# Attention and MLP decode on one core: the last 64 rows of w2 move from a load beside wq into the K/V stream, as eight strided loads, and the last w1 block streams 4 columns instead of 64

## The chip, the cores and the metric

One core of a Trainium2 chip. The metric is the device time of one execution in microseconds (us). The profile's *span* runs from the first to the last recorded instruction and is 1.3 to 1.5 us shorter than the time in most runs; I call the difference, time less span, the **outside time**.

## The reference

```python
# x: 4 x 1 x 640; k_cache, v_cache: 4 x 32 x 4096 x 128 (bf16); wq 640 x 4096; wo 4096 x 640
# w1 640 x 1728; w2 1728 x 640
def _A_ref(x, k_cache, v_cache, wq, wo):          # cached attention, one query row a batch
    q = (x @ wq).reshape(B, Sq, H, Dh) ...
    scores = jnp.einsum("bhqd,bhkd->bhqk", q, k_cache) * (Dh ** -0.5)
    o = jnp.einsum("bhqk,bhkd->bhqd", softmax(scores), v_cache)
    return o ... @ wo
def _B_ref(x, w1, b1, w2):                        # mish MLP
    h = x @ w1 + b1
    return (h * jnp.tanh(softplus(h))) @ w2
h = x + _A_ref(layernorm(x), k_cache, v_cache, wq, wo)
out = h + _B_ref(layernorm(h), w1, b1, w2)
```

Nearly all of the bytes are K and V: 32 tiles of 8 MB out of 283 MB. F = 1728 is 13 blocks of 128 rows and a rest of 64; this rest (FT = 64 rows of w2, 80 KB) is what the change moves.

## The kernel before

`sp`, `ac`, `pe` and `dv` below are the programs of SyncE, ScalarE, TensorE (PE) and VectorE. `load(p, dst, src, key, sem)` starts a DMA on engine `p`; `need(key)` waits for it. Three 8 MB buffers (slots A, B, C) take the K and V tiles in turn, all from SP's queue.

```python
def first_loads():
    load(sp, slot["C"][:, 0 : DC * H * Dh], A_wq..., "wq", "WQ")      # 5.2 MB
    load(ac, x_bf[:, :], x_rows[:, :], "x", "X")
    load(ac, w2_tail[0:FT, :], B_w2[FM * P : F, :], "w2t", "WT")      # 64 rows x 1280 bytes
    k_load(0)
    k_load(1)

def sync_prog():
    for hg in range(NHG):
        i = hg * N
        ...                                                           # cut
        sp.need(("PV", i - 1) if hg else "b1p")                       # b1p: b1 transposed by PE
        v_load(i)
        sp.need(("F", i, NS - 1))
        k_load(i + 2)
        ...                                                           # cut: the other tiles, then wo, w1, w2
```

The end of PE's program: w1 in three column blocks (2, 2 and 1 of the five 128-row chunks of D), then the part of w2 that needs only the residual, then the w2 products. WD = 16 makes PE write each result 16 times (64 columns for 4 rows of data); only one copy is read. The extra columns keep PE busy: the last block's 14 products take 1.08 us with 64 columns at clock 0.5.

```python
    for c0, c1 in zip(W1S, W1S[1:]):                                  # (0,2) (2,4) (4,5)
        ...                                                           # cut: b1 before the last block
        pe.need(("w1", c0))
        for j in [FM] + list(range(FM)):
            for c in range(c0, c1):
                ...                                                   # cut: w is the 128 x 128 piece of w1
                mm(h1_w[0 : (P if j < FM else FT), j, :, :], w,
                   cen[:, c, :].unsqueeze(1).to_broadcast([P, WD, N]), False, done, ...)
    pe.need("h_lo", "h_hi")
    ...                                                               # cut: 40 small products, the residual
    pe.need("act")
    pe.need("w2t")
    w2_mm(FM)                                                         # the 64-row rest
    for j0, j1 in zip(W2S, W2S[1:]):                                  # blocks 0-3, 4-7, 8-11, 12
        pe.need(("w2", j0))
        for j in range(j0, j1):
            w2_mm(j)
```

The softmax here doesn't subtract the row's maximum and nothing guards it: scores larger than these inputs give would overflow.

Of the kernel before, what the change touches and what calls it, by code (L numbers as in the profile page):

```python
# [78 lines left out]
def kernel(  # L79
# [15 lines left out]
    N, _, D = A_x.shape  # L95
    _, H, Sk, Dh = A_k_cache.shape
    F = B_w1.shape[1]
    P = 128
    DC = D // P
# [8 lines left out]
    FM = F // P  # L108
    FT = F - FM * P
# [22 lines left out]
    def sb(name, shape, dt, region=at, top=SLOT0):  # L132
        size = 4 if dt == FP32 else 2
        for d in shape[1:]:
            size *= d
        size = -(-size // 32) * 32
        t = nc.alloc_sbuf_tensor_at(name, shape, dt, offset=region[0]).ap()
        region[0] += size
        assert region[0] <= top, (name, region[0])
        return t  # L140
# [29 lines left out]
    w2_tail = sb("w2_tail", (P, D), BF16)  # L170
# [32 lines left out]
    cen = sb("cen", (P, DC, N), BF16, tail, topA)  # L203
# [24 lines left out]
    WD = 16  # L228
# [9 lines left out]
    h1_w = red[:, 2:4, :].rearrange("p k (j w n) -> p (k j) w n", w=WD, n=N)  # L238
# [13 lines left out]
    sp = Prog(nc.sync, book)  # L252
    po = Prog(nc.gpsimd, book)
    ac = Prog(nc.scalar, book)
    dv = Prog(nc.vector, book)
    pe = Prog(nc.tensor, book, take=["DVP", "DVA", "ACP", "VA", "VC", "V2"] + WSEM + ["B0", "B1"])

    def tiles(src, i):
        hg, b = divmod(i, N)
        return src[b, hg * G : (hg + 1) * G].rearrange("h (q r) d -> (h q) (r d)", q=PG)  # L260

    def load(p, dst, src, key, sem):
        p.do(lambda: p.eng.dma_start(out=dst, in_=src), key, sem, 16)  # L263
# [22 lines left out]
    def k_load(i):  # L286
        c = KS[i % N]
        load(sp, slot[c][:, :], tiles(A_k_cache, i), ("K", i), "K" + c)

    def v_load(i):  # L290
        c = VS[i % N]
        src = tiles(A_v_cache, i)
        n = SLOT // 2 if i == NT - 1 else SLOT
        load(sp, slot[c][:, 0:n], src[:, 0:n], ("V", i), "V" + c)
        if n < SLOT:
            load(sp, slot[c][:, n:SLOT], src[:, n:SLOT], ("V2", i), "V2")
        elif i % N == N - 1:
            sp.signal(("V2", i), "V2", 16)

    def first_loads():  # L300
        load(
            sp, slot["C"][:, 0 : DC * H * Dh], A_wq.rearrange("(p c) n -> p (c n)", c=DC), "wq", "WQ"
        )
        load(ac, x_bf[:, :], x_rows[:, :], "x", "X")
        load(ac, w2_tail[0:FT, :], B_w2[FM * P : F, :], "w2t", "WT")
        k_load(0)
        k_load(1)

# [3 lines that stand above are left out]
            if hg:  # L312
                sp.need(("PV", i - 2))
                k_load(i)
                sp.need(("F", i - 1, NS - 1))
                k_load(i + 1)
            sp.need(("PV", i - 1) if hg else "b1p")
            v_load(i)
            sp.need(("F", i, NS - 1))
            k_load(i + 2)  # L320
            sp.need(("PV", i))
            v_load(i + 1)
            sp.need(("F", i + 1, NS - 1))
            k_load(i + 3)
            sp.need(("F", i + 2, NS - 1))
            v_load(i + 2)
            sp.need(("PV", i + 1))
            v_load(i + 3)
        sp.need(("F", NT - 1, NS - 1))
        for n, (q, j0, j1) in enumerate(WOS):  # L330
            load(
                sp, wo_sb[:, q, j0:j1, :],
                A_wo[q * QN : (q + 1) * QN, :].rearrange("(p j) n -> p j n", j=G)[:, j0:j1, :],
                ("wo", q, j0), f"W{n}",
            )
        w1_v = B_w1.rearrange("(p c) n -> p c n", c=DC)
        for k, (c0, c1) in enumerate(zip(W1S, W1S[1:])):
            load(sp, w1_sb[:, c0:c1, :], w1_v[:, c0:c1, :], ("w1", c0), f"W{len(WOS) + k}")
        sp.need(("PV", NT - 2))
        for k, (j0, j1) in enumerate(zip(W2S, W2S[1:])):  # L340
            load(
                sp, w2_sb[:, j0:j1, :],
                B_w2[j0 * P : j1 * P, :].rearrange("(p j) n -> p j n", j=j1 - j0), ("w2", j0),
                f"W{len(WOS) + len(W1S) - 1 + k}",
            )
        store(sp, 0)
        leave(sp, 0)
# [378 lines left out]
    def mm(out_, lhsT, rhs, start, stop, mark=None, skip=True):  # L726
        pe.do(
            lambda: nc.tensor.matmul(  # L728
                out_, lhsT=lhsT, rhs=rhs, start=start, stop=stop, skip_group_check=skip
            ),  # L730
            mark, "PE",
        )
# [100 lines left out]
    def l_mm(hg):  # L833
        pe.need(("rsm", hg))
        mm(l_ps, rsm[:, :, :].rearrange("p b g -> p (b g)"), ones[:, :], True, True, ("L", hg))
# [34 lines left out]
    def pe_tail():  # L870
        def wo_mm(k):
            pe.need(("a", k))
            for j in range(G):
                if (k, j) in [w[:2] for w in WOS]:
                    pe.need(("wo", k, j))
                for c in range(DC):
                    w = wo_sb[:, k, j, :].rearrange("p (m c) -> p c m", c=DC)[:, c, :]
                    done = k == NHG - 1 and j == G - 1 and c == DC - 1
                    mm(
                        y_w[:, c, :, :], w, a_t[:, k, j, :].unsqueeze(1).to_broadcast([P, WD, N]),  # L880
                        False, done, "y" if done else None,
                    )

        hg = NHG - 1
        pe.freeze()
        wo_mm(0)
        o_mm(NT - 1)
        l_mm(hg)
        wo_mm(1)
        a_mm(hg)  # L890
        pe.need("zeros", ("e", NT - 1, NS - 1))
        for k in (2, 3):
            mm(red[:, k, :], ident[:, :], zeros[:, 0:1].to_broadcast([P, 512]), True, False)
        mm(y2_ps, ident[:, :], zeros[:, 0:OC], True, False)
        wo_mm(2)
        wo_mm(3)
        pe.need("ysum")
        mm(m_ps, ones_d[:, :], ysum[:, :], True, True, "mean")
        pe.need("sq")
        mm(sq_ps, ones_d[:, :], sq[:, :, :].rearrange("p c n -> p (c n)"), True, True, "sqm")  # L900
        pe.need("cen")
        for c0, c1 in zip(W1S, W1S[1:]):
            if c1 == DC:
                pe.need("b1_lo")
                for part in (b1_hi, b1_lo):
                    for j0, j1 in ((0, FC // 2 + 1), (FC // 2 + 1, FC)):
                        mm(h1_ps[:, j0:j1, :], ident[:, :], part[:, j0:j1, :], False, False)
# [3 lines that stand above are left out]
                    if j < FB * FI:  # L911
                        k, i = divmod(j, FI)
                        w = w1_sb[:, c, k * FI * P : (k + 1) * FI * P]
                        w = w.rearrange("p (f i) -> p i f", i=FI)[:, i, :]
                    else:
                        w = w1_sb[:, c, j * P : min((j + 1) * P, F)]
                    done = c == DC - 1 and j == FM - 1
                    mm(
                        h1_w[0 : (P if j < FM else FT), j, :, :], w,
                        cen[:, c, :].unsqueeze(1).to_broadcast([P, WD, N]), False, done,  # L920
                        "h1_ps" if done else None,
                    )
        pe.need("h_lo", "h_hi")
        for part in (h_hi, h_lo):
            for k in range(CG):
                for c in range(DC):
                    mm(
                        y2_ps[k * QD : k * QD + N, :].rearrange("b (m c) -> b c m", c=DC)[:, c, :],
                        part[:, c, :], ident[:, k * QD : (k + 1) * QD], False, False,
                    )  # L930
        pe.need("act")

        def w2_mm(j):
            rows = P if j < FM else FT
            for k in range(CG):
                cs = slice(k * OC, (k + 1) * OC)
                done = j == FM - 1 and k == CG - 1
                mm(
                    y2_ps[k * QD : k * QD + N, :], act[0:rows, j, :],
                    w2_sb[:, j, cs] if j < FM else w2_tail[0:FT, cs], False, j == FM - 1,  # L940
                    "y2" if done else None,
                )

        pe.need("w2t")
        w2_mm(FM)
        for j0, j1 in zip(W2S, W2S[1:]):
            pe.need(("w2", j0))
            for j in range(j0, j1):
                w2_mm(j)
# [77 lines left out]
```

## Time and profile before

The first three runs gave a median of 661.48 us (661.27 to 661.50).

The page of the kernel before: its span, the granted TensorE clock (PEclk, tenths of full speed), the DMA rows over 40 equal slices, the queues (packets, MB, share; q1 is SP's, q10 is ACT's) and the chain of waits that ended last.

```profile
span 659.9 us, 4968 instructions
...
PEclk9768787979759697958767888788875879796968
DMA  9999999999999999999999999999999999999997
GB/s 387 445 445 441 434 406 437 442 441 434 430 417 445 437 437 433 437 417 445 433 441 433 437 417 445 433 437 438 433 421 445 429 437 441 433 421 445 415 416 324
...
q1 hardware_dynamic: 6784, 283.27, 99.4%
...
q10 hardware_dynamic: 112, 0.09, 0.0%
...
DMA 3%; SPq 2%; PE 1%; issue 0%; DVE 0%
DMA slotA<-in_B_w_dram 3%; SPq L263 2%; PE pv L728 1%; PE red L738 0%; PE red L728 0%; DVE o_bf L724 0%
```

The DMA row is full in 39 of 40 slices and the stream moves 429 to 430 GB/s; 27.1 GB/s for each of 16 DMA engines. The chain is the end of that stream. So the time is the stream, plus a start, plus a tail. Two loads, from the view of DMA issues (KB each, us from issue to landing):

```profile
slotC<-in_A_wq_dram SPq DMA_DIRECT2D x1, 5120.0 KB, 16.0
...
w_tail<-in_B_w_dram ACTq DMA_DIRECT2D x1, 80.0 KB, 13.3
```

The tail, from the timeline (start us, busy us, engine, line, operation, tile, shape, count, and in brackets the idle time before it and what ended it):

```profile
651.32 1.64 PE L728 MATMUL red<-cen,slotB 128*64 128x64 bf16 x28 [0.78 <-DMA slotB<-in_B_w_dram]
...
652.99 1.08 PE L728 MATMUL red<-cen,slotB 128*64 128x64 bf16 x14
...
655.65 0.22 DVE L717 SCALAR_TENSOR_TENSOR act<-tb,hm 128x56 bf16<-128x56 f32 x1
...
655.92 0.24 PE L728 MATMUL red<-w_tail,act 64*4 64x160 bf16 x4 [1.09 <-DVE act L717]
...
656.09 0.72 PE L728 MATMUL red<-slotA,act 128*4 128x160 bf16 x32
...
657.02 0.65 PE L728 MATMUL red<-slotA,act 128*4 128x160 bf16 x20 [0.21 <-DMA slotA<-in_B_w_dram]
...
657.73 0.32 DVE L724 CAST o_bf<-red 128x160 bf16<-128x160 f32 x1 [1.86 <-PE red L728]
```

`cen` products are w1's, `act` is the activation, `slotA,act` products are w2's, `o_bf` is the output copy. PE runs 32 w2 products, then waits for the last w2 loads. The chain says so too:

```profile
639.18 17.80 DMA slotA<-in_B_w_dram
...
657.02 0.68 PE red L728 x20
```

And the granted clock over the tail, from the view by windows (length, then busy time and count by engine, PEclk, DMA share, GB/s):

```profile
core 0: us, PE busy (x) PEld busy (x) DVE busy (x) ACT busy (x) POOL busy (x), PEclk, DMA share, GB/s
651.40:654.10 2.70, 2.70 (x54) 2.47 (x58) 0.00 (x0) 0.00 (x0) 0.00 (x0) 0.56 1.02 420
654.10:655.90 1.80, 0.73 (x40) 0.54 (x38) 1.54 (x6) 0.25 (x1) 0.00 (x0) 0.71 0.93 374
655.90:658.10 2.20, 1.54 (x56) 0.93 (x56) 0.32 (x1) 0.00 (x0) 0.00 (x0) 1.00 0.19 73
```

PEclk is 0.56 during the last w1 blocks and 1.00 during the w2 products.

Below I also use the trace's packet records, which no printed view lists one by one. Sorted by end, the 64 KB packets of K and V fall into groups of 16, one packet for each DMA engine, so the lag of every engine at every step can be read, although the engines carry no names. In this stream a group follows the last after 2.415 us, within 0.01 us, except where an instruction fetch or a small load falls between: whatever an engine loses, it keeps to the end. The last w2 load therefore lands when the *slowest* engine has its share: first landing 655.70 us, last 657.39 us.

### The profile page before, as it was taken

The numbers are of one execution on the slowest core, as the hardware profiler recorded it, in microseconds if no ns is written. First come the engines' busy times: TensorE is split into PE (matmuls) and PEld (weight loads), VectorE is DVE, ScalarE is ACT, GpSimd is POOL, SyncE is SP. The second block draws the span as 40 slices with busy tenths as digits, with TensorE's granted clock in tenths as the row PEclk, the third lists the DMA queues.
The fourth block names the chain that finished last, engine by engine and source line by source line (L and its number), as shares of the span: only waits on it lengthen the run. The fifth ranks groups of instructions, "written<-read, shape, count | busy, mean of one in ns | idle before, by whom it ended". The sixth has DMA issues, their size and how long they took to land. (4 is left out here: it accounts for less than half of the span.)

```text
span 659.9 us, 4968 instructions
## 1 busy us (share of the span) xinstructions
PE 382.4 (58%) x2630; PEld 68.6 (10%) x1672; DVE 407.7 (62%) x257; ACT 40.7 (6%) x157; POOL 1.7 (0%) x12
## 2 busy tenths in 40 slices
PE   0356758556317595738417485848434757675766
PEld 0100000101101010101100010010110001010145
DVE  1077988495049778757208798849306798857702
ACT  0200000000000000000000000000000000000011
POOL 0000000000000000000000000000000000000000
PEclk9768787979759697958767888788875879796968
DMA  9999999999999999999999999999999999999997
GB/s 387 445 445 441 434 406 437 442 441 434 430 417 445 437 437 433 437 417 445 433 441 433 437 417 445 433 437 438 433 421 445 429 437 441 433 421 445 415 416 324
DMA packets 6905, 283.48 MB, mean 430 GB/s; under 512 B 809, under 2 KB 1136, under 8 KB 2160
## 3 DMA queue, kind: packets, MB, share of 16 engines
q1 hardware_dynamic: 6784, 283.27, 99.4%
q8 instruction: 6, 0.10, 0.1%
q10 hardware_dynamic: 112, 0.09, 0.0%
q14 instruction: 3, 0.02, 0.0%
HBM read 283.35 MB, written 0.01 MB: 429 GB/s over the span
## 5 line engine op out<-in xcount | busy, mean ns | idle before, releaser
L527 DVE TENSOR_TENSOR slotA<-slotA,q_bc 128x8192 bf16<-128x8192 bf16 x32 | 140.6, 4415 | 92.2 <-DMA slotA<-in_A_k_cache_dram 92.2
L527 DVE TENSOR_TENSOR slotB<-slotB,q_bc 128x8192 bf16<-128x8192 bf16 x32 | 140.7, 4416 | 16.2 <-DMA slotB<-in_A_k_cache_dram 16.2
L538 DVE TENSOR_REDUCE s_f<-red 128x64 f32<-128x1024 f32 x64 | 78.0, 1219 | 96.4 <-PE red L738 96.3
L738 PE MATMUL red<-slotA,ident 128*128 128x512 bf16 x480 | 137.3, 450 | 0.0
L738 PE MATMUL red<-slotB,ident 128*128 128x512 bf16 x480 | 124.5, 418 | 0.0
L728 PE MATMUL red<-slotA,ident 128*128 128x512 bf16 x32 | 14.5, 452 | 128.5 <-PEq L49 128.5
L728 PE MATMUL pv<-slotC,e 128*32 128x512 bf16 x768 | 51.9, 430 | 39.6 <-PEq L49 36.6
L728 PE MATMUL red<-slotB,ident 128*128 128x512 bf16 x32 | 14.0, 437 | 86.9 <-PEq L49 86.9
L404 ACT ACTIVATE ex<-s_f 128x64 bf16<-128x64 f32 x64 | 16.4, 256 | 511.4 <-DVE s_f L538 511.4
L552 DVE TENSOR_TENSOR e<-ex,hmask 128x512 bf16<-128x512 bf16 x64 | 39.8, 683 | 0.0
L728 PEld LDWEIGHTS pv<-slotC,e 128*32 128x32 bf16 x768 | 22.3, 107 | 97.7 <-issue 83.6
L728 PEld LDWEIGHTS red<-slotA,ident 128*128 128x128 bf16 x32 | 3.2, 99 | 197.2 <-issue 197.1
L728 PEld LDWEIGHTS red<-slotB,ident 128*128 128x128 bf16 x32 | 3.1, 98 | 169.0 <-issue 169.0
L728 PEld LDWEIGHTS o_ps<-pv_sb,selo 128*32 128x32 f32 x136 | 13.5, 109 | 63.6 <-issue 63.5
L728 PE MATMUL o_ps<-pv_sb,selo 128*32 128x128 f32 x136 | 18.0, 276 | 0.0
L728 PE MATMUL pv<-slotA,e 128*32 128x512 bf16 x256 | 14.5, 379 | 0.9 <-PEq L49 0.9
L414 ACT COPY pv_sb<-pv 128x512 f32<-128x512 f32 x16 | 9.4, 585 | 70.6 <-PE pv L728 70.6
L404 ACT ACTIVATION_READ_ACCUMULATOR ex<-s_f 128x1 f32 x64 | 11.9, 186 | 0.0
L577 DVE RECIPROCAL rl<-misc 32x1 f32<-32x1 f32 x4 | 0.6, 151 | 14.4 <-PE misc L728 14.4
L728 PEld LDWEIGHTS pv<-slotA,e 128*32 128x32 bf16 x256 | 7.1, 97 | 22.2 <-issue 16.6
L517 DVE CAST b1T<-pv 128x13 bf16<-128x13 f32 x1 | 0.2, 174 | 13.1 <-PE pv L728 13.1
L728 PE MATMUL red<-slotC,lnT 128*32 128x512 bf16 x40 | 4.4, 620 | 6.0 <-PEq L49 6.0
(105 smaller groups left out, 70.3 us busy)
## 6 DMA issues: line engine op xcount, KB each, us to landing
slotC<-in_A_v_cache_dram SPq DMA_DIRECT2D x2, 4096.0 KB, 40.5
slotC<-in_A_wq_dram SPq DMA_DIRECT2D x1, 5120.0 KB, 16.0
slotB<-in_A_wo_dram SPq DMA_DIRECT2D x3, 1280.0 KB, 17.7
slotA<-in_B_w_dram SPq DMA_DIRECT2D x3, 640.0 KB, 18.9
slotB<-in_B_w_dram SPq DMA_DIRECT2D x2, 864.0 KB, 24.4
slotB<-in_A_wo_dram SPq DMA_DIRECT2D x1, 640.0 KB, 21.4
slotB<-in_A_wo_dram SPq DMA_DIRECT2D x1, 480.0 KB, 22.1
slotB<-in_B_w_dram SPq DMA_DIRECT2D x1, 432.0 KB, 22.8
```

The costliest lines, as they stand in the source:

```text
L404: lambda: a.activation(out=ex[:, sl], in_=s_f[:, sl], func=ACT.Exp, scale=SCALE, accum_out=rs[:, b, s : s + 1],),
L414: lambda: a.copy(out=pv_sb[:, :, :].rearrange("p r d -> p (r d)"), in_=pv[:, :]),
L517: dv.do(lambda: v.tensor_copy(out=b1T[:, 0:FM], in_=b1_ps[:, 0:FM]), "b1m", DV)
L527: lambda: v.tensor_tensor(out=t, in0=t, in1=q_bc[:, hg, b, :].unsqueeze(1).to_broadcast([P, RS, Dh]), op=ALU.mult,),
L538: lambda: v.tensor_reduce(out=s_f[:, s * RS : (s + 1) * RS], in_=red[:, k : k + 2, :].rearrange("p k (r c) -> p (k r) c", c=CW), axis=AX.X ...
L552: lambda: v.tensor_tensor(out=e[:, sl, :], in0=ex[:, sl].unsqueeze(2).to_broadcast([P, RS, G]), in1=hmask[:, :].unsqueeze(1).to_broadcast( ...
L577: dv.do(lambda: v.reciprocal(out=rl[:, :], in_=l_ps), ("rl", hg), DV)
L728: lambda: nc.tensor.matmul(out_, lhsT=lhsT, rhs=rhs, start=start, stop=stop, skip_group_check=skip),
L738: return t.add_instruction(mybir.InstMatmult(name=nc.get_next_instruction_name(), engine=mybir.EngineType.PE, ins=[t.lower_ap(rhs), t.lowe ...
```

## The change

Intent: take the 80 KB away from the start, where they compete with wq, and load them later in the stream, in eight loads of eight rows, each at every fourth partition. And shorten PE's last w1 block, so that a shorter DMA stream isn't followed by PE work.

```diff
@@ first_loads
-        load(ac, w2_tail[0:FT, :], B_w2[FM * P : F, :], "w2t", "WT")
@@ sync_prog, after v_load(i)
+            if hg == 0:
+                for k in range(FT // 8):
+                    r = slice(k // 4 * 32 + k % 4, k // 4 * 32 + 32, 4)
+                    load(sp, w2_tail[r, :], B_w2[FM * P : F, :][r, :], ("w2t", k), "WT")
@@ last w1 block
+                    wd = WD if c1 < DC else 1
                     mm(
-                        h1_w[0 : (P if j < FM else FT), j, :, :], w,
-                        cen[:, c, :].unsqueeze(1).to_broadcast([P, WD, N]), False, done,
+                        h1_w[0 : (P if j < FM else FT), j, 0:wd, :], w,
+                        cen[:, c, :].unsqueeze(1).to_broadcast([P, wd, N]), False, done,
@@ before the w2 products
-        pe.need("w2t")
+        pe.need(("w2t", FT // 8 - 1))
```

## The prediction

> **What bounds the kernel.** The page shows 283.48 MB at 430 GB/s, the DMA row at 9 tenths in 39 of 40 slices; PE is busy 58%, DVE 62%. The trace's packet records, followed one by one, are sharper: from 1.2 to 657 us no DMA engine is without work, and every 64 KB packet of the K and V stream takes 2.418 us (27.1 GB/s an engine). So the span is start-up, the bytes of the *slowest* of 16 engines, and what follows the last landing. The chain of waits agrees: it ends in the w2 loads, then w2 products (0.68 us), output copy (0.32 us) and store. The engines are out of step: the last w2 load lands on its first engine 1.69 us before its last. Small loads of x and b1 leave three engines up to 1.2 us late, and each instruction fetch (8 or 16 KB, at 80, 97, 118, 147, 157, 176, 457 us) sets one engine back by about 0.6 to 1.5 us.
>
> **What changes.**
> 1. w2's last 80 KB leave the start. There every engine carried four 1280-byte packets, each 52 to 66 ns between two wq packets, plus a completion: about 0.25 us. All 16 engines should start the K stream that much earlier.
> 2. The same bytes come back behind V tile 0. [...] this trace can't name engines, but the four-row x load has four data landings. Those engines get eight packets and eight completions, estimated from the packets above at 0.42 to 0.5 us; the rest none. Net: engines 0 to 7 about +0.2 us, 8 to 15 about -0.25 us.
> 3. Eight more issues cost SP about 8 x 0.43 us near 23 us, where it next waits until about 60 us: free.
> 4. The 14 products of the last w1 block take 1.08 us at half clock with 64 columns; with 4 I estimate 0.5 us. But PE already waits for the last two w2 landings (idle 0.21 and 0.17 us before them), so this is off the path, or insurance should the DMA end earlier.
>
> **On the path.** Only the slowest engine counts. The four latest lie within 0.25 us. If all are among 8 to 15, the end moves by -0.25 us; if one is among 0 to 7, by 0 to +0.25 us. The trace does not say which; I take it as even. Fewer columns could also lower the granted clock for the w2 products (a few tenths of a us).
>
> **Prediction:** 661.35 us, eight times in ten within 660.8 to 661.9. Faster by over 2%: 1%; within 2%: 98%; slower: 1%.
>
> **What would show it.** wq lands about 0.2 us earlier; eight 10 KB loads on SP follow V tile 0; K landings shift by -0.2 us before them, half the engines by +0.2 afterwards; the last w1 products take about 0.5 us; PE idle before the last w2 landings grows to 0.5 us or more; the chain still ends in w2 loads.
>
> **What would make it wrong.** wq packets slow from 1.514 to 1.645 us at about 8 to 11.5 us on all engines at once; if w2's load causes this, another 0.3 us is won. Small packets that stall a 64 KB neighbour would cost more. Fetches that fall on other engines would move the maximum by up to 0.5 us.

"Those engines" and "engines 0 to 7" are the eight that I took to carry the eight loads, "8 to 15" the rest; the trace numbers none. The sum came to 0.13 us under the 661.48 us of before, which is even odds of -0.25 us and of about 0.

## The result

In the first comparison the changed kernel took 661.83 us (median of 6, 661.55 to 663.01), the kernel before 661.49 us (6 runs): ratio 1.0008, interval 0.9996 to 1.0021. A ratio here is the mean time of one kernel's fast runs over that of the other's of the same rounds, so not quite the ratio of the medians. Three repeats gave 1.0009, 1.0010 and 1.0004. Each interval holds 1; the four together say "slower by a few tenths of a us", against the 0.13 us faster that I forecast.

The page after:

```profile
span 660.2 us, 4975 instructions
...
PEclk9768787968659796868767887788876879797967
...
q1 hardware_dynamic: 6912, 283.35, 99.3%
...
q10 hardware_dynamic: 32, 0.01, 0.0%
...
DMA 4%; PE 2%; SPq 0%; DVE 0%; issue 0%; ACT 0%
DMA slotB<-in_B_w_dram 4%; PE red L731 1%; PE pv L731 1%; PE red L741 0%; SPq L263 0%; DVE tb L717 0%; DVE o_bf L727 0%; ACT ta L441 0%; DVE tb L706 0%; DVE h L694 0%; DVE act L720 0%; DVE tb L714 0%
```

The DMA issues after:

```profile
slotC<-in_A_wq_dram SPq DMA_DIRECT2D x1, 5120.0 KB, 15.5
...
w_tail<-in_B_w_dram SPq DMA_DIRECT2D x8, 10.0 KB
```

The first step of the forecast is there: wq lands 0.5 us sooner after its issue (15.5 for 16.0 us), and the eight 10 KB loads are on SP. The tail, from the timeline:

```profile
651.46 1.82 PE L731 MATMUL red<-cen,slotB 128*64 128x64 bf16 x28 [0.80 <-DMA slotB<-in_B_w_dram]
...
653.32 0.73 PE L731 MATMUL red<-cen,slotB 128*64 128x4 bf16 x14
...
655.63 0.22 DVE L720 SCALAR_TENSOR_TENSOR act<-tb,hm 128x56 bf16<-128x56 f32 x1
...
655.90 0.30 PE L731 MATMUL red<-w_tail,act 64*4 64x160 bf16 x4 [1.09 <-DVE act L720]
...
656.13 1.90 PE L731 MATMUL red<-slotA,act 128*4 128x160 bf16 x52
658.09 0.33 DVE L727 CAST o_bf<-red 128x160 bf16<-128x160 f32 x1 [2.24 <-PE red L731]
```

The chain:

```profile
626.18 25.24 DMA slotB<-in_B_w_dram
...
651.46 2.60 PE red L731 x46
...
655.90 2.16 PE red L731 x55
```

And the clock over the tail:

```profile
core 0: us, PE busy (x) PEld busy (x) DVE busy (x) ACT busy (x) POOL busy (x), PEclk, DMA share, GB/s
651.40:654.10 2.70, 2.64 (x55) 2.51 (x59) 0.01 (x1) 0.00 (x0) 0.00 (x0) 0.52 1.02 422
654.10:655.90 1.80, 0.71 (x40) 0.52 (x36) 1.52 (x6) 0.25 (x1) 0.00 (x0) 0.50 0.84 336
655.90:658.10 2.20, 2.14 (x56) 1.51 (x56) 0.01 (x1) 0.00 (x0) 0.00 (x0) 0.50 0.16 61
```

Three things are new. The last w1 block is shorter, 0.73 for 1.08 us, and yet the activation comes at the same time (655.63 and 655.65 us), because the second block started later and ran slower. The clock is then 0.50 where it was 1.00, and the 52 w2 products run for 1.90 us without waiting for the last loads: PE, not the stream, now ends the kernel, and the output copy starts at 658.09 instead of 657.73 us. And the chain, which was the w2 load followed by PE, is now the second w1 load followed by PE, ScalarE and VectorE. The last w2 landing itself moved by only 0.14 us, to 657.53 us.

That looks like a complete story, 0.36 us of it. It isn't: it is one profile of each kernel, and the repeats below show that the *spans* of the two kernels do not differ on average.

### The profile page after: what moved, and what is told of

It is laid out like the page before. It is cut to its first block, busy times and chain, and to the rows that moved or that the text cites. A ratio compares the mean times of both kernels' runs of the same rounds, so it can differ in the third digit from the quotient of the medians.

```text
span 660.2 us, 4975 instructions
## 1 busy us (share of the span) xinstructions
PE 388.8 (59%) x2630; PEld 69.5 (11%) x1672; DVE 407.8 (62%) x257; ACT 40.7 (6%) x157; POOL 1.7 (0%) x12
## 5 line engine op out<-in xcount | busy, mean ns | idle before, releaser
L741 PE MATMUL red<-slotA,ident 128*128 128x512 bf16 x480 | 140.4, 458 | 0.0
L741 PE MATMUL red<-slotB,ident 128*128 128x512 bf16 x480 | 126.1, 422 | 0.0
L731 PE MATMUL red<-slotA,ident 128*128 128x512 bf16 x32 | 14.3, 448 | 127.4 <-PEq L49 127.4
L731 PE MATMUL red<-slotB,ident 128*128 128x512 bf16 x32 | 14.1, 440 | 85.3 <-PEq L49 85.3
## 6 DMA issues: line engine op xcount, KB each, us to landing
slotC<-in_A_wq_dram SPq DMA_DIRECT2D x1, 5120.0 KB, 15.5
```

The source lines that it names most:

```text
L731: lambda: nc.tensor.matmul(out_, lhsT=lhsT, rhs=rhs, start=start, stop=stop, skip_group_check=skip),
L741: return t.add_instruction(mybir.InstMatmult(name=nc.get_next_instruction_name(), engine=mybir.EngineType.PE, ins=[t.lower_ap(rhs), t.lowe ...
```

## The experiments

All runs in one table. "Ratio" is to the kernel before in the same call. "Long" counts the runs with an outside time (time less span, 1.3 to 1.5 us in most runs) above 1.7 us. For the kernel before I pool 46 runs: mean time 661.77 us, mean span 660.26 us (659.7 to 661.0), 4 of 46 long; a 47th, of 822.84 us, was slow and is left out, and so are the six runs of the first comparison, for which no spans are on record. Spans are recorded to 0.1 us, so runs close to 1.7 us can fall on either side of that line.

| run | what | median us | ratio | spans us | long |
|---|---|---|---|---|---|
| after | the change | 661.83 | 1.0008 | 660.1 to 660.4 | 4 of 6 |
| r1 | the same | 662.51 | 1.0009 | 660.1 to 660.2 | 5 of 6 |
| r3 | the same | 661.93 | 1.0010 | 660.2 to 660.5 | 3 of 5 |
| r6 | the same | 661.68 | 1.0004 | 660.1 to 660.4 | 1 of 5 |
| e1 | stream, wide block | 661.62 | 1.0000 | 659.9 to 660.7 | 0 of 5 |
| r4 | the same | 661.94 | 1.0004 | 660.0 to 660.8 | 0 of 5 |
| e2 | narrow block only | 661.56 | 0.9998 | 660.1 to 660.3 | 0 of 5 |
| r5 | the same | 661.45 | 1.0001 | 659.9 to 660.5 | 0 of 5 |
| e3 | stream, one load | 661.60 | 0.9997 | 659.8 to 660.2 | 1 of 5 |
| e6 | stream, four loads | 661.32 | 0.9995 | 659.7 to 660.6 | 0 of 6 |
| e4 | rest not loaded | 661.35 | 0.9996 | 659.4 to 660.1 | 1 of 5 |
| e5 | start, eight loads | 666.22 | 1.0066 | 663.8 to 665.2 | 2 of 6 |
| e7 | start, before x | 661.78 | 1.0001 | 659.9 to 660.7 | 1 of 6 |
| f1 | changed, 24 spare products | 661.75 | 1.0003 | 660.2 to 660.4 | 0 of 5 |
| f3 | changed, 4 spare products | 661.72 | 0.9999 | 660.1 to 660.4 | 0 of 5 |
| f2 | before, 20 products fewer | 661.64 | 0.9999 | 659.8 to 660.5 | 0 of 5 |
| g1 | four loads, wide, 14 spare wide products | 661.15 | 0.9991 | 659.7 to 659.9 | 0 of 5 |
| g2 | the same | 661.13 | 0.9989 | 659.6 to 660.1 | 0 of 5 |
| g3 | before, 14 spare wide products | 661.33 | 0.9990 | 659.7 to 660.0 | 0 of 5 |

The lag of the DMA engines, worked out from the packet records of each profile: mean end of the first K packet over the 16 engines; mean time lost behind V tile 0, against eight undisturbed packets; end of the 241st of the 248 groups of 64 KB packets on the slowest engine; last w2 landing.

| profiles | first K packet | lost behind V0 | slowest at the end | last w2 landing |
|---|---|---|---|---|
| one load beside wq (before, e2, r5, e7, f2, g3) | 17.00 to 17.12 | 0.00 | 598.19 to 598.34 | 657.34 to 657.50 |
| eight in the stream (after, r1, r3, r6, f1, f3, e1, r4) | 16.48 to 16.58 | 0.34 to 0.38 | 598.30 to 598.35 | 657.46 to 657.53 |
| one in the stream (e3) | 16.51 | 0.46 | 598.35 | 657.51 |
| four in the stream (e6, g1, g2) | 16.48 to 16.53 | 0.39 to 0.41 | 598.11 to 598.25 | 657.26 to 657.40 |
| none (e4) | 16.58 | 0.00 | 597.83 | 656.97 |

### The two halves apart: e1 and e2, with r4 and r5

e1 (and r4) restore the wide block and keep the stream; e2 (and r5) do the reverse.

```diff
# e1, r4: changed kernel
-                    wd = WD if c1 < DC else 1
+                    wd = WD
# e2, r5: kernel before
+                    wd = WD if c1 < DC else 1
# (and 0:wd, [P, wd, N] in the product, as in the change)
```

> The changed kernel with 64 columns restored in the last w1 block; w2's last rows stay in the stream. Theory A (the narrow block keeps the clock window from 651.5 us on at 0.5, and the slow w2 products then end the kernel): the window after about 655 us is granted 1.0 again as before, the 52 w2 products take about 1.4 us instead of 1.90, the end follows the last w2 landing (657.5 us, which does not move) and the span is 660.0 to 660.1, 0.1 to 0.2 us shorter than the changed kernel's 660.15. Rival (the phase of the clock window is luck, columns do not matter): the clock at the end is 0.5 or 1.0 independently of the columns, span 660.1 to 660.2 with 0.5.

> The kernel before with only the last w1 block narrowed to 4 columns; w2's last rows stay beside wq. Theory A: the clock stays at 0.5 from about 651.7 us to the end, w2 products about 1.9 us, output copy at about 658.0 instead of 657.73, span 0.2 to 0.3 us over the kernel before; the landings of K, V and w2 stay as before (last w2 at about 657.4), and wq packets again slow to about 1.645 us between 8 and 11.5 us. Rival (luck of the window): clock 1.0 at the end in this one, span within 0.1 us of before.

> Stream placement with the wide last block, again (it differs from the changed kernel in the last block's columns alone). If the long outside time belongs to the new load on SP alone: above 1.7 here too. If it needs the narrow block: about 1.4 as in the first five runs (1.35 to 1.43). Clock at the end: 1.0 if the columns set it, either if the window's phase does (the one-load run with wide columns had 0.5).

> The narrow last block with w2's rows beside wq, again. If the long outside time belongs to the narrow block alone: above 1.7 in most runs; the first five gave 1.36 to 1.69, so I expect about 1.4 to 1.6, and the clock at 0.5 after about 655 us (columns) in this third profile of a narrow kernel; a clock of 1.0 there would be the first against it.

e1 went as theory A said: clock 1.0 from 655.1 us, w2 products 1.48 us, output copy at 657.81 us, span of the profiled run 659.9 us. e2 too: clock 0.5 from 649.2 us on, products 1.91 us, copy at 657.97 us. But r4, the same program as e1, had the clock at 0.5 from 650.0 us to the end, and its tail is slower than the changed kernel's:

```profile
653.30 1.08 PE L731 MATMUL red<-cen,slotB 128*64 128x64 bf16 x14
...
656.47 1.90 PE L731 MATMUL red<-slotA,act 128*4 128x160 bf16 x52
658.42 0.33 DVE L727 CAST o_bf<-red 128x160 bf16<-128x160 f32 x1 [2.24 <-PE red L731]
```

The copy starts at 658.42 us, later than in the changed kernel (658.09), and that profiled run's span was 660.6 us. r5, the same program as e2, had 1.0 from 653.2 to 656.6 us and only then 0.5. So neither theory is right alone. Over all profiles without wide spare products, the clock was 1.0 through the w2 products in 7 of 9 profiles with the wide block (not in r4 and e3), and at 0.5 for all of them in 7 of 8 with the narrow one (f1 and f3 counted, r5 in part). All clock records but the one cut off by the end last whole multiples of 3.41 us, which I call windows (before: 1.0 from 638.09 us, 0.5 from 651.75, 1.0 from 655.16, 0.5 from 658.57), and their phase differs from run to run (the rise at 638.09 us in before is at 637.83 in the changed kernel). What PE has to do to be granted 1.0 the traces do not show. By the counts above, columns set the odds. What decides the single run is not shown; the window's phase alone does not: e3 and e6 are both wide and their clocks rose within 0.1 us of each other (638.48 and 638.55 us), yet e3 fell to 0.5 at 652.1 us and e6 stayed at 1.0 to 659.0 us.

The price of each case can be read off the copy's start: wide and clock 1.0, 657.73 us (before; 657.71 to 657.84 with e1, e6, e7 and f2); narrow and 0.5, 658.01 to 658.09 (changed, four profiles); wide and 0.5, 658.08 (e3, where the clock fell only at 652.1 us) and 658.42 (r4). The narrow block exchanges a mixture of the first and the last for the middle, nearly always. The spans fit this, though only one of the runs of before was profiled: the 22 of the changed kernel lie within 660.1 to 660.5 (standard deviation 0.10, mean 660.22 us), the 46 of before within 659.7 to 661.0 (0.31, mean 660.26 us). The mean did not move.

### What the 80 KB cost where: e3, e4 and e6

```diff
# e3: changed kernel, wide block, one load behind V tile 0
+                load(sp, w2_tail[0:FT, :], B_w2[FM * P : F, :], "w2t", "WT")
# e6: the same with four loads of 16 rows
+                for k in range(FT // 16):
+                    r = slice(k, FT, 4)
+                    load(sp, w2_tail[r, :], B_w2[FM * P : F, :][r, :], ("w2t", k), "WT")
# e4: kernel before without the load; rows of w2's first block in their place
-        load(ac, w2_tail[0:FT, :], B_w2[FM * P : F, :], "w2t", "WT")
```

> w2's last rows in the stream behind V tile 0, but as one 64-row load over 16 engines; last w1 block 64 columns. Theory A (in the stream only packets count: each engine gets four 1280-byte packets and one completion, about 0.25 us, and no engine 0.7): the slowest engine at the last K packets is 0.3 to 0.5 us earlier than in the changed kernel, last w2 landing near 657.0 to 657.2, span 659.6 to 659.8. Rival [...]: the eight or sixteen engines lose 0.7 us or more behind V tile 0 and the span is 660.1 or more.

> WRONG RESULT ON PURPOSE: w2's last rows are not loaded at all (rows of the first w2 block are used in their place); last w1 block 64 columns. It measures what the 80 KB cost in each place. Theory A: wq packets stay at 1.514 us, the K stream starts 0.5 to 0.7 us earlier than before, no engine loses time behind V tile 0, and the last w2 landing is 0.5 to 0.7 us earlier than before (656.7 to 656.9); the products then wait less, span 659.3 to 659.5. Rival (the slow wq packets of before were chance or another user of memory): wq packets slow to 1.645 us here too, span only about 0.25 us under before.

> w2's last rows in the stream behind V tile 0 as four 16-row loads (every fourth partition), four packets and four completions on each of 16 engines; last w1 block 64 columns. The one-load run showed every engine losing about 0.54 us there for four packets, the eight-load runs eight engines losing about 0.68 for eight. Theory A [...]: the fastest engines again lose about 0.5 us or more behind V tile 0. Rival (the loss of the one-load run is its four rows on one engine in a row, or a fixed cost of a small load): each engine loses about 4 x 0.085 = 0.34 us, and the last w2 landing is about 0.2 us earlier than in the one-load run (657.3). Span in either case 659.8 to 660.2, not to be told from before.

e4 is wrong by design; the comparison with the reference let it pass all the same, since these 64 rows add too little to the output. It gives the ceiling: without the 80 KB the last landing is at 656.97 us, 0.4 us earlier (I had expected 0.5 to 0.7), and spans are 659.4 to 660.1 us. In every profile without the load beside wq the wq packets take a flat 1.514 us.

e3 missed theory A: four packets and one completion cost an engine 0.46 us in the stream on average (the fastest 0.53), not 0.25, and the last landing stayed at 657.51 us. e6, with as many packets for each engine but in four loads, cost 0.41 us, between the two expectations; its last landing (657.40 us) is 0.1 us earlier. The eight loads of the change cost 0.35 us as a mean over 16 engines. The sorted lags before and after V tile 0 fit eight engines that hardly change and eight that fall back (in r4, eight of the sixteen lags come back within 0.01 us); the whole loss on eight is 0.35 x 16 / 8 = 0.70 us each. The landing records agree with eight engines for a load of eight rows: 8 data landings for each of the eight loads, 16 for e3's one load, 4 for the four-row load of x.

So a 1280-byte row, 0.047 us at 27.1 GB/s, costs 0.09 to 0.12 us between 64 KB packets, its share of the completions included (0.70 / 8, 0.41 / 4, 0.46 / 4). Placement in the stream is not free, and no arrangement of these three is better than another by more than about 0.15 us at the last landing (means: eight loads 657.49, one 657.51, four 657.35 us).

### The start: e5 and e7

```diff
# e5: kernel before
-        load(ac, w2_tail[0:FT, :], B_w2[FM * P : F, :], "w2t", "WT")
+        for k in range(FT // 8):
+            r = slice(k // 4 * 32 + k % 4, k // 4 * 32 + 32, 4)
+            load(ac, w2_tail[r, :], B_w2[FM * P : F, :][r, :], ("w2t", k), "WT")
# e7: kernel before, w2t issued before x
-        load(ac, x_bf[:, :], x_rows[:, :], "x", "X")
         load(ac, w2_tail[0:FT, :], B_w2[FM * P : F, :], "w2t", "WT")
+        load(ac, x_bf[:, :], x_rows[:, :], "x", "X")
```

> w2's last rows stay at the start on the ACT queue beside wq, but as the eight 8-row loads; last w1 block 64 columns. It separates the shape of the load from its place. Theory A (the slow wq packets of before and of the narrow-only run, 1.58 to 1.65 us, come from the place, whatever the shape): wq packets slow again, or the laggards again start the K stream 0.5 us later than in the runs without w2 beside wq (last wq landing 15.8 to 16.1 rather than 15.4). Rival [...]: wq packets flat at 1.514 us, wq lands by about 15.5 on the engines that carry none of the eight loads.

> The kernel before, with w2's 64-row load issued first on the ACT queue and the x load second. Idea: its packets reach the engines while the first wq packets still wait 2.2 to 2.7 us for their data, so part of them is free; x lands some 0.6 us later, which nothing waits for (wq lands 10 us later). Theory: K stream starts 0.2 to 0.4 us earlier than before, last w2 landing 657.0 to 657.2, span 659.5 to 659.8. Rival (packets of the two queues alternate one for one, so w2's still fall between the first five wq packets, and slow the later ones just as before): no change, wq packets slow to 1.6 us, last w2 landing at 657.4.

The slow wq packets come with the shape. In all six profiles with the 64-row load beside wq, the wq packets slow down at about 8 to 11.5 us, to a median of 1.61 to 1.71 us at the worst; in e5, with the same bytes at the same place in eight strided loads, all stay at 1.514. So the eight-row shape avoids the slowing. What in the 64-row shape causes it is not shown: all 16 engines slow down, the slowing begins 4 us after the load's first packets, and in the stream the four loads of e6 are not clearly worse than the eight of the changed kernel (0.41 us lost behind V tile 0 against a mean of 0.35, last landing 657.40 against 657.49). e7 gained nothing (ratio 1.0001, wq packets up to 1.71 us): its rival held.

e5 also cost 4.4 us, which neither theory had. In the kernel before, PE transposes b1 at 22 us and SP then starts V tile 0:

```profile
22.24 0.29 PE L728 MATMUL pv<-ident,b1r 3*128 3x3 bf16 x4
...
22.70 0.33 SPq L263 DMA_DIRECT2D slotC<-in_A_v_cache_dram  x1
```

In e5:

```profile
44.21 0.26 PE L730 MATMUL pv<-ident,b1r 3*128 3x3 bf16 x4 [21.34 <-PEq L49]
...
44.67 0.33 SPq L263 DMA_DIRECT2D slotC<-in_A_v_cache_dram  x1
```

b1's two loads stand behind eight loads in ACT's queue, and that queue gets one packet for each 64 KB packet of SP's: the last piece of b1 lands at 44.08 us instead of 20.47. V tile 0 is issued 22 us late and the stream falls short of work. This alternation shows in the eight w2 loads' landings in e5: on one engine they come about 1.5 us apart beside the 40 KB packets of wq, and 2.4 to 2.5 us apart beside the 64 KB packets. So in e5, beside the stream of 64 KB packets, a tiny load waited 2.4 us for each packet ahead of it in its own queue. In the kernel before, less than 2 us (20.47 to 22.24) separated b1 from being late.

### The time outside the span: r1, r3, r6, f1, f2 and f3

> The changed kernel again, unedited, for a second profile and a second comparison of five rounds. Theory A (the change costs about 0.3 us: 0.1 from the slowest engine, 0.2 from w2 products at half clock): ratio to before again above 1.0003, the clock at the end 0.5 again with about 1.9 us of w2 products, and the wq packets at a flat 1.514 us. Rival theory B (both kernels spread over about 0.8 us from run to run, by start-up offsets of the engines, fetches and the phase of the clock window, and the 0.3 us of the first comparison was drawn from that spread): ratio within 0.0005 of 1 on either side, spans of before and changed overlapping (659.8 to 660.6).

> The changed kernel a third time. So far its span (12 runs: 660.1 to 660.4) is no longer than that of the kernel before (19 runs: 659.8 to 660.7), while its time outside the span (time less span) is above 1.7 us in 9 of 12 runs and at most 1.7 in 18 of 19 runs of before. Theory A (a trait of the changed kernel): outside time again above 1.7 in most of these runs, ratio again about 1.0005 to 1.0010, span within 0.2 of before's mean. Rival (drawn by chance in two sittings): outside time about 1.4, ratio within 0.0003 of 1.

> The changed kernel a fourth time. Expected if its excess is a trait: ratio 1.0005 to 1.0012, span 660.1 to 660.3, outside time above 1.7 us in more than half of the runs. If the profiled run has an outside time above 1.7, a 16 KB fetch begins after the span's end; if it is below 1.45, that fetch is at about 658 or not in the record. Rival: outside time about 1.4 throughout.

r1 and r3 make plain luck unlikely, and rule out theory A of r1: spans are no longer than those of before, so the excess isn't in the DMA engines or the w2 products. Over the 22 runs of the changed kernel the mean time is 662.14 us, 0.37 over before; the mean span is 0.04 us *under*; the outside time is 1.92 us against 1.51. 13 of 22 are long, 4 of 46 before (above 1.9 us: 10 and 3; the longest are 2.81 us in the changed kernel and 3.08 in before). r6 showed it more weakly (1 of 5, one more at 1.69). Neither half alone has it: none of 10 runs of the stream with the wide block, none of 10 of the narrow block alone. The long outside time isn't the changed kernel's alone, though: e3, e4, e5 and e7 have 5 long runs of 22. Nor is the chip ruled out as a part of it: r1 and r3 ran on one chip (8 of 11 long), r6 on another (1 of 5), and no run separates them.

The packet records give a companion. Instructions come in by fetches of 8 and 16 KB (3 and 6 of them within the span of before). The 16 KB ones are taken to be PE's, since added PE products move them (below), and one belongs to the very end:

| profile | outside time of that run | last 16 KB fetch starts |
|---|---|---|
| r1 | 2.13 | 661.46 (span 660.2) |
| e5 | 1.97 | 665.76 (span 664.5) |
| r3, r6, e1, e2, e3, e7, r4 | 1.34 to 1.43 | 657.9 to 658.1 |
| before, after, e4, e6, r5, f2 | 1.35 to 1.43 | none recorded after 654 |

The two profiled runs with a long outside time are the two in which a fetch starts about 1.3 us after the span's end. To test it I moved the fetch: spare products of zeros into an unread bank, in gaps where PE waits.

```diff
# f1: changed kernel; f3: only the second place, range(4)
             if c0 == 2:
+                for _ in range(12):
+                    mm(red[0:32, 1, 0:4], ident[:, 0:32], zeros[:, 0:4], True, True)
             pe.need(("w1", c0))
 ...
+        for _ in range(12):
+            mm(red[0:32, 1, 0:4], ident[:, 0:32], zeros[:, 0:4], True, True)
         pe.need("act")
# f2: kernel before without the low part of the residual (slightly wrong on purpose)
-        for part in (h_hi, h_lo):
+        for part in (h_hi,):
```

> The changed kernel with 24 four-column products of zeros added in gaps in which PE waits anyway (12 before the second w1 block, 12 before the activation), results untouched. Both profiles with a long outside time (1.97 and 2.13 us) show a 16 KB instruction fetch that starts 1.3 us after the span's end; the other eight have none there and 1.36 to 1.43 us. Theory A (this late fetch is what the changed kernel pays; where it falls depends on how many instructions PE has run): the added instructions move the fetch of PE's last block before the end, outside time falls to about 1.4 in all runs, and the time is 0.5 us under the changed kernel's of the same call. Rival (the outside time has another cause, the fetch only accompanies it): outside time stays above 1.7 in most runs.

> The changed kernel with 4 tiny products of zeros before the activation (f1 had 24). Theory A: the fetch starts 8 instructions earlier in PE's order, at about 657.8 us by the pace of the w2 products, always before the end, and the outside time is 1.35 to 1.45 in all runs. Rival (f1's cure came from something else than the shift, its busier PE for instance): outside time still above 1.7 in half of the runs or more.

> SLIGHTLY WRONG RESULT ON PURPOSE: the kernel before without the 20 products that add the low part of the residual (about 40 PE instructions fewer). Theory A (the last fetch starts at a fixed PE instruction close to the end; pushed past the end, it lengthens what comes after the span): the fetch near 658 us is gone from inside the span, and the outside time rises above 1.7 us in most runs, span unchanged or 0.1 us shorter. Rival (the fetch is not the cause, or is then not needed at all): outside time 1.3 to 1.5 as in before.

f1 and f3 held in kind: the fetch starts at 656.8 us and 657.19 us, and the outside time is 1.35 to 1.41 in five of five runs and 1.37 to 1.52 in five of five. Mean times fall by 0.36 us against r3 and 0.24 us against r6, the changed kernel, while the spans do not fall (660.34 for 660.28, 660.26 for 660.26). The gain is all outside. f3 does it with four tiny products, which leave the clock at 0.5 as it was. f2 missed: a shorter PE program has no late fetch and no long outside time (1.34 to 1.43). So "any program that ends early in the fetched block pays" is refuted. What stands: with a few PE instructions added, none of 10 runs is long, where the changed kernel in the same two calls has 4 of 10 (3 of 5 against f1, but only 1 of 5 against f3, so f3 alone proves little); and in both profiles that caught the long outside time, a late fetch was there. What stays open is why the fetch is late in some runs of this kernel and not in e1 or e2, which have as many PE instructions, and whether the fetch causes the wait or goes with it.

### A version from the findings: g1, g2 and g3

Wide spare products in the same gaps keep PE busy (for the clock) and lengthen its program (for the fetch). g1 and g2 add them to e6, g3 to the kernel before and nothing else.

```diff
             if c0 == 2:
+                for _ in range(6):
+                    mm(red[:, 1, 0:P], ident[:, :], ident[:, :], True, True)
             pe.need(("w1", c0))
 ...
+        for _ in range(8):
+            mm(red[:, 1, 0:P], ident[:, :], ident[:, :], True, True)
         pe.need("act")
```

> The version that the experiments point to: w2's rows as four 16-row loads behind V tile 0, the wide last block, and 14 spare 128-column products in gaps where PE waits (6 before the second w1 block, 8 before the activation), to keep the clock at 1.0 and the last fetch early. Expected: clock 1.0 from about 650 us to the last w2 product in most profiles, products waiting for the last landing (657.3 to 657.4), output copy at 657.7, span 659.7 to 660.0, outside time 1.35 to 1.45, time 661.1 to 661.4, ratio 0.9993 to 0.9998: at the edge of what five rounds can tell. Rival (the clock follows the window's phase whatever PE does, or the spare products delay the second w1 block): half clock at the end, span 660.1 or more, ratio 1.0000 or above.

> g1 again, unedited. If its gain is real: median 661.0 to 661.4, spans 659.7 to 660.0, outside time below 1.5, ratio 0.9988 to 0.9996, clock 1.0 during the last w2 products. If it was drawn by luck: spans scattered over 659.7 to 660.6 as the kernel before, ratio 0.9997 to 1.0003.

> The kernel before with the same 14 spare products and nothing else. If the gain of g1 comes from the clock and the fetch: as g1 (median 661.0 to 661.4, spans 659.7 to 660.0, never 660.5), since the last w2 landing of before (657.4) equals that of the four-load version. If it comes from the four-load placement: spans scattered 659.8 to 660.7 as before, median 661.5 to 661.8.

The rival of g1 fell. All three have the clock at 1.0 during the w2 products; g3's tail and clock:

```profile
653.13 1.08 PE L728 MATMUL red<-cen,slotB 128*64 128x64 bf16 x14
...
656.23 1.40 PE L728 MATMUL red<-slotA,act 128*4 128x160 bf16 x52
...
657.68 0.32 DVE L724 CAST o_bf<-red 128x160 bf16<-128x160 f32 x1 [1.67 <-PE red L728]
```

```profile
core 0: us, PE busy (x) PEld busy (x) DVE busy (x) ACT busy (x) POOL busy (x), PEclk, DMA share, GB/s
651.40:654.10 2.70, 2.70 (x46) 2.48 (x46) 0.00 (x0) 0.00 (x0) 0.00 (x0) 0.50 1.04 425
654.10:655.90 1.80, 1.32 (x50) 1.05 (x48) 1.43 (x6) 0.25 (x1) 0.00 (x0) 0.87 0.85 346
655.90:658.10 2.20, 1.54 (x56) 0.93 (x56) 0.43 (x2) 0.00 (x0) 0.00 (x0) 1.00 0.21 76
```

The copy is at 657.68 us, as in the good case of before, and the bad case did not appear: 15 spans of 15 are at most 660.1 us, where before ranged over 659.7 to 661.0 (means 660.28 and 660.37). Ratios 0.9991, 0.9989 and 0.9990. Each interval still holds 1 (0.9977 to 1.0005, 0.9975 to 1.0002, 0.9977 to 1.0004); it is the three together, and the spans, that make it convincing. g3 has w2's rest still beside wq: nearly all of the gain (0.6 to 0.8 us in mean time) comes with the spare products: 0.5 to 0.6 us of it in the span, as the steady clock and tail would give, and 0.1 to 0.2 us outside it. Moving the load is worth about the 0.1 us between the means of g2 and g3, which is not clear of the noise.

## Why the prediction was wrong

I forecast 661.35 us, 0.13 under before; it came out at 661.83, and four comparisons put it 0.3 to 0.7 us over before (the ratios times 661.5). "Within 2%" was right, and so was the bound up to the tail: the stream and its slowest engine. The step that failed is **"Only the slowest engine counts"**, with step 4's "so this is off the path": the slowest engine ended 0.09 us later, as I had allowed for, but the products that I had put off the path ended the span at half clock, and the excess of 0.37 us in the mean time lies after the span, where my sum had no term (outside time 1.92 us instead of 1.51). Step by step:

- **Step 1, "about 0.25 us ... All 16 engines should start the K stream that much earlier".** Right in kind, half the size: the mean start moved from about 17.04 us (mean of the six profiles with the load beside wq) to 16.52, so 0.52 us. Of this, the slow wq packets account for about 0.3 us (in before, the medians over 1.514 add up to 0.32). I had named them as what might add "another 0.3 us", and it did; e4 and e5 show that they belong to the 64-row load. That three engines were late because of the loads of x and b1 was wrong or at least unsupported: the latest one was late from its first wq packet on, which ended at 4.45 us.
- **Step 2, "estimated from the packets above at 0.42 to 0.5 us".** Mis-sized: 0.70 us on eight engines. Packets between 40 KB packets at the start do not price packets between 64 KB packets in the stream.
- **"Net: engines 0 to 7 about +0.2 us".** Gain and cost were both forecast too small by about 0.25 us, so this held by cancellation: 0.70 - 0.52 = 0.18. The branch "if one is among 0 to 7, by 0 to +0.25 us" is the one that came: slowest engine about 0.09 us later (mean of the eight profiles with eight loads, 598.33, less that of the six with the load beside wq, 598.24), last landing 657.46 to 657.53 us. What sets this maximum stands in the packet records: in six of the eight profiles with eight loads the lag of the slowest engine rises by 0.5 to 0.7 us across the 8 KB instruction fetch at 455 to 457 us; until then it was on average 0.24 us earlier than in the six with the load beside wq. I had named the fetches as what might move the maximum by 0.5 us, and left them out of the sum.
- **Step 3, the issues on SP are free.** Right; they took 0.62 us each instead of 0.43, and nothing waited.
- **Step 4, "so this is off the path".** This is the step that failed inside the span. The last w1 block did get shorter (0.73 us, not 0.5), but with less work PE was granted 0.5 instead of 1.0 in all four profiles of the changed kernel, the w2 products took 1.9 us or more, and PE became the end of the chain. I had written "could also lower the granted clock for the w2 products (a few tenths of a us)" and then gave it no weight in the sum. I also took the kernel before to have clock 1.0 at its end always, from one profile. Two other kernels with the wide block lost it (e3, r4), and the spread of before's spans suggests that it does too at times; that would be why the mean span is unchanged (660.22 against 660.26 us).
- **What the sum did not contain.** The measured excess, 0.37 us over 22 runs, lies outside the span: 1.92 less 1.51 is 0.41 us. My sum ended with the last store. That the excess lies there is shown by the runs; its cure by a few PE instructions is likely (none of 10 runs long); its mechanism stays open.

So the expected 0.13 us, and the 0.5 us that the start really gained, went three ways: given back behind V tile 0 on the engines that carry the eight loads, put behind a PE tail at half clock in every profile of the changed kernel, and lastly paid for after the last store.

## What to carry to other kernels

When every DMA engine is always busy, work out a change per engine and look at the slowest: moving small loads shifts cost between engines and gains nothing unless the slowest sheds it, and here a row of 1280 bytes between 64 KB packets cost about twice what its bytes alone would take (0.09 to 0.12 us for 0.047). Don't trim "useless" PE columns just before a tail that PE must finish quickly without looking at the granted clock: here it was 0.5 for all of the w2 products in 7 of 8 profiles with the narrow block and 1.0 in 7 of 9 with the wide one, and at 0.5 they took 1.90 us or more, at 1.0 in f2 1.40 us. Here a few spare products in idle gaps made the clock (1.0 in all three profiles), and with it the span (at most 660.1 us in 15 of 15 runs), steady and were worth more than the change. Before believing a difference of 0.1%, compare spans as well as times over repeats: one pair of profiles told a clean story that the mean of the spans did not bear out.
